# Transposing q, k, phi and x of the first six chunks on TensorE instead of by DMA

## The chip, the cores and the metric

One core of one Trainium2 chip runs the kernel. The metric is the device time of one execution in us. A profile holds one execution; its span goes from the first to the last instruction, and the execution's own time is somewhat longer.

## What is computed

q, k and v have shape (4, 8, 576, 64): four batches, eight heads, 576 positions, 64 features, float32. Attention with a memory is followed by two feed-forward layers over 2304 tokens (4 x 576) of width 512 (8 x 64):

```
scores = scale * q @ k^T, causal; a = softmax(scores); local = a @ v
q_p = phi(q), phi(x) = elu(x) + 1
mem_out = (q_p @ M_prev) / (q_p . z_prev + 1e-6)
x = g * mem_out + (1 - g) * local          # g = sigmoid(beta) per head
x = softplus(x @ moe_w_in) @ moe_w_out     # 512 -> 2048 -> 512
out = relu(x @ moe2_w_in)^2 @ moe2_w_out   # 512 -> 2048 -> 512
```

## The kernel before

**Precision.** Nearly every float32 operand is split in two 16-bit halves, a rounded one (hi) and the rest (lo), and the products are put together in PSUM. ScalarE makes hi with a Copy, VectorE makes lo with a subtraction.

**Chunks.** The tokens form 18 chunks of 128 (`g` = 0 to 17), nine for each pair of batches. For a chunk, `prep_k`, `prep_q`, `prep_phi` and `prep_v` (lines 201 to 247) take the loaded float32 tile, split it and bring it into the layout in which the features lie on partitions. For k, a head's 64 hi and 64 lo features stand side by side, so one 128 x 128 transpose per head gives `KT`. For q two orders are needed, hi-lo and lo-hi, as the score is the sum of (hi, lo) by (hi, lo) and of the swapped order: `qn` (line 203) has both orders, the second made by two VectorE copies (lines 206 and 207), and 16 blocks are transposed into `qT`. phi has eight blocks (`phiT`), x eight (`xT`), four of hi and four of lo.

**Transposes.** `transp(g, out, in_, lim)` (lines 186 to 199) has two routes. For `g >= lim` SP issues DMA transposes from SBUF to SBUF, 16 blocks in two halves, fewer at once (line 192). For `g < lim` TensorE transposes each block of 128 columns against an identity into a PSUM tile `tps` of eight blocks (line 198), and ScalarE copies the tile to SBUF (line 199). `TQ` is 2: q, k, x and the probabilities of chunks 0 and 1 go over TensorE, all later ones by DMA. phi has limit 0 and always goes by DMA.

**A chunk's attention.** A step is a group of one to four heads (`steps`, line 499). `emit_s` (lines 273 to 309): TensorE writes scores into the single tile `s_ps` (line 298), VectorE adds the mask and finds the row's extreme (line 302), ScalarE takes the exponential and its sum (line 306). `emit_p` (lines 311 to 325) splits the probabilities `Pt` into `p` (lines 319 and 320) and transposes them into `PT`. Four steps later (`LAG`) `emit_pv` (lines 327 to 344) multiplies `PT` by `V` and `phiT` by `Mt` into `pvt`; `prep_n` (line 249) makes the memory's norm. `emit_x` (lines 349 to 373) weighs and adds the two, splits x into `xn` and transposes it into `xT`, from which the first feed-forward layer reads. `attn_step` (line 535) emits the preparation of chunk g + 1 in four parts spread over the steps of chunk g.

**Feed-forward.** A block is two chunks (256 tokens). `unit_h` (line 411) multiplies `xT` by `W1` (`hps`, lines 421 to 423) and applies softplus on ScalarE and VectorE (lines 425 to 432); `unit_x` (line 444) and, for block 0, `unit_xq` (line 466) multiply by `W2`. The first layer's weights come in 32 pieces that are loaded by SP (lines 384 and 387) and split by VectorE and ScalarE (lines 403 to 408) while attention starts. The second layer (from line 681) follows when the first is done.

**What sets the order.** Each engine runs its own stream in order, and SP's queue issues loads, weight pieces and DMA transposes in order. A hand-written planner (lines 595 to 650) interleaves attention steps with units of feed-forward work from a queue, by estimated costs, and a scheduler orders each engine's stream when the program is built, by priorities set around `emit_s`, `emit_p`, `emit_x` and the weight pieces. PSUM has eight banks: `s_ps` two, `pvt` one, the accumulators of block 0 two, and `mm` three buffers, which `tps`, `nps` and `hps` share (line 96) until block 0 is done.

Of the kernel before, what the change touches and what calls it, by code (L numbers as in the profile page):

```python
# [9 lines left out]
F16 = mybir.dt.float16  # L10
# [3 lines left out]
AF = mybir.ActivationFunctionType  # L14
ALU = mybir.AluOpType
AX = mybir.AxisListType

P = 128
# [7 lines left out]

LOE = 99
TQ = 2
GPL = 0
W34P = 0  # L30

# [11 lines left out]
def kernel(  # L43
# [15 lines left out]
    pe, act, dve, pool, sp = nc.tensor, nc.scalar, nc.vector, nc.gpsimd, nc.sync  # L59
    B, H, S, D = q.shape  # L60
# [43 lines left out]
    att = att_cm.__enter__()  # L104
    sps = sps_cm.__enter__()
    pvp = pv_cm.__enter__()
    mm = mma_cm.__enter__()
# [25 lines left out]
    ident = stage.tile([P, P], F16, name="ident", bufs=1)  # L133
# [21 lines left out]
    raw, qT, phiT, KT, V, Mt, Pt, PT, pvt, cs_t = ({} for _ in range(10))  # L155
# [11 lines left out]
    def lo_eng(g):  # L167
        return dve if g < LOE else pool
# [17 lines left out]
    def transp(g, out, in_, lim):  # L186
        nblk = in_.shape[1] // P
        if g >= lim:
            step = nblk if nblk <= 12 else nblk // 2
            for a in range(0, nblk, step):  # L190
                e = a + step
                sp.dma_start_transpose(out=out[:, a:e], in_=in_[:, a * P:e * P])
            return
        for a in range(0, nblk, 8):
            e = min(nblk, a + 8)
            ps = mm.tile([P, 8, P], F16, tag="mm", name="tps")
            for i in range(a, e):
                pe.transpose(ps[:, i - a], in_[:, i * P:(i + 1) * P], ident)
            act.activation(out[:, a:e], ps[:, :e - a], AF.Copy)  # L199

    def prep_q(g):
        r = raw["q", g]
        qn = att.tile([P, 2, H, 2, D], F16, name="qn")
        act.activation(qn[:, 0, :, 0, :], r, AF.Copy)
        lo_eng(g).tensor_tensor(qn[:, 0, :, 1, :], r, qn[:, 0, :, 0, :], ALU.subtract)
        dve.tensor_copy(qn[:, 1, :, 1, :], qn[:, 0, :, 0, :])
        dve.tensor_copy(qn[:, 1, :, 0, :], qn[:, 0, :, 1, :])
        qT[g] = att.tile([P, 2 * H, P], F16, name="qT", bufs=2)
        transp(g, qT[g], qn.rearrange("p a h t d -> p (a h t d)"), TQ)

    def prep_k(g):
        r = raw.pop(("k", g))
        kn = att.tile([P, H, 2, D], F16, name="kn")
        act.activation(kn[:, :, 0, :], r, AF.Copy)
        lo_eng(g).tensor_tensor(kn[:, :, 1, :], r, kn[:, :, 0, :], ALU.subtract)
        KT[g] = att.tile([P, H, P], F16, name="KT", bufs=KVB)
        transp(g, KT[g], kn.rearrange("p h t d -> p (h t d)"), TQ)

    def prep_v(g):
        r = raw.pop(("v", g))  # L220
# [15 lines left out]
    def prep_phi(g):  # L236
        r = raw.pop(("q", g))
        e = att.tile([P, H, D], F32, tag="prod", name="phie")
        act.activation(e, r, AF.Relu, scale=-1.0)
        act.activation(e, e, AF.Exp, scale=-1.0)  # L240
        f = att.tile([P, H, D], F32, name="phi")
        dve.scalar_tensor_tensor(f, r, 0.0, e, ALU.max, ALU.add)
        fn = att.tile([P, H, 2, D], F16, name="phin")
        act.activation(fn[:, :, 0, :], f, AF.Copy)
        lo_eng(g).tensor_tensor(fn[:, :, 1, :], f, fn[:, :, 0, :], ALU.subtract)
        phiT[g] = att.tile([P, H, P], F16, name="phiT", bufs=2)
        transp(g, phiT[g], fn.rearrange("p h t d -> p (h t d)"), 0)

    def prep_n(g):
        ps = mm.tile([P, H], F32, tag="mm", name="nps")  # L250
# [60 lines left out]
    def emit_p(g, h0):  # L311
# [10 lines left out]
        nblk = G * 2 * w // P  # L322
        transp(g, t[:, :nblk], t16[:, :G * 2 * w], TQ)
        for i in range(G):
# [21 lines left out]
    xT = {}  # L346
    xf_t = {}

    def emit_x(g, a):
        kb, off = divmod(g * P, NB)  # L350
        if off == 0 and a == 0:
            xT[kb] = w1p.tile([P, 2 * NCC, NB], F16, name="xT", bufs=2)
        hs = slice(a * H // 2, (a + 1) * H // 2)
        cc = cc_t[g]
        c1 = cc[:, a, 0, :]
        dve.tensor_scalar(c1, cs_t[g][:, 1, hs], 1.0e-9, None, ALU.add)
        dve.reciprocal(c1, c1)
        dve.tensor_tensor(c1, c1, gP[:, hs], ALU.mult)
        t = att.tile([P, 2, H // 2, D], F32, tag="prod", name="xt")
        dve.tensor_tensor(  # L360
            t, pvt.pop(g),
            cc[:, a].rearrange("p t (h o) -> p t h o", o=1).to_broadcast([P, 2, H // 2, D]), ALU.mult,
        )
        if a == 0:
            xf_t[g] = att.tile([P, H, D], F32, name="xf")
        xf = xf_t[g]
        dve.tensor_tensor(xf[:, hs], t[:, 0], t[:, 1], ALU.add)
        if a == 0:
            return
        xn = att.tile([P, 2, H, D], F16, name="xn")  # L370
        act.activation(xn[:, 0], xf, AF.Copy)
        dve.tensor_tensor(xn[:, 1], xf, xn[:, 0], ALU.subtract)
        transp(g, xT[kb][:, :, off:off + P], xn.rearrange("p t h d -> p (t h d)"), TQ)


    NPC = 16
# [36 lines left out]
    def unit_h(kb, fp):  # L413
# [17 lines left out]
        act.activation(g[0], a, AF.Copy)  # L431
        (pool if fp % 8 < GPL else dve).tensor_tensor(g[1], a, g[0], ALU.subtract)  # L432

# [68 lines left out]
    def prep_part(g, part):  # L502
        if g >= NC:
            return
        if part == 0:
            prep_k(g)
            load("k", g + 1)
        elif part == 1:
            prep_q(g)
        elif part == 2:  # L510
            prep_phi(g)
            load("q", g + 1)
        elif part == 3:
            prep_v(g)
            load("v", g + 1)
            prep_m(g)
            load_m(g + 1)

    prep_k(0)
    prep_q(0)  # L520
    prep_phi(0)
    prep_v(0)
    load_m(0)
# [11 lines left out]
    def attn_step(s):  # L535
        if s < len(steps):
            g, h = steps[s]
            G = GRP[g % CPP]
            with tc.high_priority(HS):
                emit_s(g, h)  # L540
            nst = H // G
            i = h // G
            for part in range(4):
                if part * nst // 4 == i:
                    prep_part(g + 1, part)
            with tc.high_priority(HP):
                emit_p(g, h)
        for g, h0 in pv_at.get(s, ()):
            for h in range(h0, h0 + GRP[g % CPP]):
                emit_pv(g, h)  # L550
                if h % 4 == 3:
                    with tc.high_priority(HXE):
                        emit_x(g, h // 4)
# [131 lines left out]
    while t0 < NT:  # L685
# [7 lines left out]
        for f in range(NFC):  # L693
            ps = mm2.tile([P, 512], F32, tag="mm2", name="h2ps")
# [7 lines left out]
            r = bp.tile([P, 512], F32, name="r2", bufs=3)  # L702
            act.activation(r[:, :n], ps[:, :n], AF.Relu, scale=u2)  # L703
            act.activation(r[:, :n], r[:, :n], AF.Square)  # L704
            g = [bp.tile([P, 512], F16, name=f"gg{t}_{f}", bufs=1) for t in range(2)]
# [5 lines left out]
        for m in range(n // P):  # L711
            ps = mm2.tile([P, 512], F32, tag="mm2", name="ops")
# [39 lines left out]
```

## Time and profile before

| | |
|---|---|
| three runs | 1002.19, 1006.45, 1006.74 us; median 1006.45 |
| the profiled execution's own time | 1002.3 us |
| its span | 1000.5 us |
| TensorE busy | 923.6 us, 92% of the span |
| VectorE busy | 594.8 us |
| ScalarE busy | 550.4 us |
| DMA queue of SP | 103.84 MB, 51.6% of 16 engines' span |

The profile names engines PE (TensorE matmuls), PEld (its weight loads), DVE (VectorE), ACT (ScalarE), POOL (GpSimd) and SP (SyncE); a q behind a name is the engine's sequencer, which issues DMAs and waits. `out<-in` are the program's tile names, L298 is line 298 of the kernel. In a group of instructions `x32` is their number, then come busy us, the mean ns of one, and the idle time before them with what ended it. The chain of waits follows the work that ended last back from the end; shares of it are of the stretch asked for. DMA share is the mean busy share of 16 DMA engines; packets can overlap, so it can be over 1. PEclk is the granted TensorE clock as a share of full speed.

### The profile page before, as it was taken

The page shows a single profiled execution, that of the slowest core. Times are in us where ns is not written, and L with a number is a line of the kernel's source. Part 1 is how long each engine was busy: PE and PEld are TensorE (multiplying, and loading weights), DVE is VectorE, ACT ScalarE, POOL GpSimd, SP SyncE. Part 2 cuts the span into 40 slices and gives each one's busy share as a digit, 9 for nine tenths or more (in the row PEclk, how much of TensorE's full clock was granted, in tenths as well). Part 3 has the DMA queues.
Part 4 walks back from the last instruction along what each step waited for, and adds up shares of the span by engine and source line. Part 5 has one row for each costly group of instructions (what it writes and reads, how often), then busy time and mean ns, then how long its engine had stood idle before and what let it go on. Part 6 is the DMA issues. An engine that isn't in the chain of part 4 may idle for free.

```text
span 1000.5 us, 21041 instructions
## 1 busy us (share of the span) xinstructions
PE 923.6 (92%) x8594; PEld 678.8 (68%) x8612; DVE 594.8 (59%) x1376; ACT 550.4 (55%) x1102; POOL 2.9 (0%) x11
## 2 busy tenths in 40 slices
PE   3557689889999999999999999999999999999998
PEld 2346578778888888988888888864444444444483
DVE  7998889876756787786757499990240141042040
ACT  7756677777848688795948374650340241043040
POOL 1000000000000000000000000000000000000000
PEclk9998889999999999999999999999999999999999
DMA  9998998894867985598545366520000000000000
GB/s 225 231 213 173 181 199 166 176 162 73 133 118 122 170 161 104 94 171 139 98 75 99 54 211 195 183 86 22 22 1 21 22 1 11 32 1 1 32 11 22
DMA packets 299953, 105.21 MB, mean 105 GB/s; under 512 B 264784, under 2 KB 297552, under 8 KB 299856
## 3 DMA queue, kind: packets, MB, share of 16 engines
q1 hardware_dynamic: 299616, 103.84, 51.6%
q8 instruction: 67, 1.10, 0.5%
q14 instruction: 30, 0.25, 0.1%
q10 hardware_dynamic: 240, 0.02, 0.0%
HBM read 48.78 MB, written 4.72 MB: 53 GB/s over the span
## 4 chain that ended last, share of the span: by engine, by line
PE 70%; DVE 13%; DMA 10%; ACT 3%; issue 3%; SPq 1%; DVEq 0%; ACTq 0%
PE ops L717 7%; PE ops L715 6%; PE ops L716 6%; PE hps L421 5%; PE hps L422 5%; PE hps L423 5%; PE h2ps L700 5%; PE h2ps L699 5%; PE h2ps L701 5%; DMA PT<-p 4%; PE s_ps L298 4%; PE xps L439 4%; PE xps L438 4%; PE xps L440 4%; PE pvt L342 2%
## 5 line engine op out<-in xcount | busy, mean ns | idle before, releaser
L706 DVE CAST gg<-r 128x512 f16<-128x512 f32 (+1 forms) x80 | 32.0, 400 | 231.3 <-ACT r L704 205.0
L421 PE MATMUL hps<-xT,W 128*128 128x256 f16 x576 | 160.5, 279 | 6.3 <-ACT xT L199 4.1
L422 PE MATMUL hps<-xT,W 128*128 128x256 f16 x576 | 160.4, 278 | 0.0
L423 PE MATMUL hps<-xT,W 128*128 128x256 f16 x576 | 160.4, 278 | 0.0
L438 PE MATMUL xps<-g,W 128*128 128x256 f16 x512 | 138.9, 274 | 2.4 <-ACT g L431 2.4
L439 PE MATMUL xps<-g,W 128*128 128x256 f16 x512 | 139.5, 274 | 0.3 <-DVE g L432 0.3
L440 PE MATMUL xps<-g,W 128*128 128x256 f16 x512 | 139.5, 273 | 0.0
L306 ACT ACTIVATE Pt<-Pt,cs 128x128 f32<-128x128 f32 (+8 forms) x144 | 87.6, 608 | 57.1 <-DVE cs L302 57.1
L298 PE MATMUL s_ps<-KT,qT 128*128 128x128 f16 (+2 forms) x992 | 89.1, 225 | 27.0 <-DVE cs L302 25.0
L717 PE MATMUL ops<-W,gg 128*128 128x512 f16 x288 | 109.2, 379 | 0.9
L715 PE MATMUL ops<-W,gg 128*128 128x512 f16 x288 | 108.7, 379 | 1.2 <-ACT W L407 1.2
L719 ACT ACTIVATE osb<-ops 128x512 f32<-128x512 f32 x18 | 10.7, 597 | 169.8 <-PE ops L717 169.8
L302 DVE CUSTOM_DVE_ANT_0 Pt<-s_ps,mask 128x128 f32<-128x128 f32 (+8 forms) x144 | 79.6, 553 | 39.7 <-PE s_ps L298 39.0
L716 PE MATMUL ops<-W,gg 128*128 128x512 bf16 x270 | 102.3, 379 | 0.0
L700 PE MATMUL h2ps<-x,W 128*128 128x512 f16 (+1 forms) x256 | 90.2, 352 | 0.0
L701 PE MATMUL h2ps<-x,W 128*128 128x512 f16 (+1 forms) x256 | 90.2, 352 | 0.0
L699 PE MATMUL h2ps<-x,W 128*128 128x512 f16 (+1 forms) x256 | 90.2, 352 | 0.0
L298 PEld LDWEIGHTS <-qT 128*128 128x128 f16 x992 | 67.1, 104 | 33.9 <-issue 28.7
L320 DVE TENSOR_TENSOR p<-Pt,p 128x512 f16<-128x512 f32 (+5 forms) x116 | 75.1, 648 | 24.7 <-ACT p L319 24.2
L703 ACT ACTIVATE r<-h2ps 128x512 f32<-128x512 f32 (+1 forms) x80 | 44.1, 551 | 71.5 <-PE h2ps L701 71.4
L342 PE MATMUL pvt<-V,PT 128*128 128x64 f16 (+1 forms) x464 | 67.1, 201 | 12.6 <-DMA PT<-p 12.6
L319 ACT ACTIVATE p<-Pt 128x512 f16<-128x512 f32 (+5 forms) x116 | 68.9, 594 | 11.2 <-DMA PT<-p 9.7
(120 smaller groups left out, 1972.4 us busy)
## 6 DMA issues: line engine op xcount, KB each, us to landing
wst<-in_moe_w_in_dram SPq DMA_DIRECT2D x32, 512.0 KB, 4.8
wst<-in_moe_w_out_dram SPq DMA_DIRECT2D x32, 512.0 KB, 4.4
out_dram<-osb SPq DMA_DIRECT2D x18, 256.0 KB, 2.0
rawk<-in_k_dram SPq DMA_DIRECT2D x16, 256.0 KB, 4.6
rawq<-in_q_dram SPq DMA_DIRECT2D x16, 256.0 KB, 4.2
rawv<-in_v_dram SPq DMA_DIRECT2D x16, 256.0 KB, 3.7
PT<-p SPq DMA_TRANSPOSE x110, 3.4
mraw<-in_M_prev_dram SPq DMA_DIRECT2D x8, 128.0 KB, 3.6
```

Of the source, the lines that this page charges most:

```text
L298: pe.matmul(o, qT[g][:, t * H + h], KT[kb][:, h, k0:k0 + e - a], start=(t == 0), stop=(t == 1),)
L421: pe.matmul(o, wh, x[:, c], start=(c == 0), stop=False)
L422: pe.matmul(o, wh, x[:, NCC + c], start=False, stop=False)
L423: pe.matmul(o, wl, x[:, c], start=False, stop=(c == NCC - 1))
L438: pe.matmul(ps, wh, gh, start=(f == f0), stop=False)
L439: pe.matmul(ps, wh, gl, start=False, stop=False)
L440: pe.matmul(ps, wl, gh, start=False, stop=(f == f1 - 1))
L699: pe.matmul(ps[:, a - t0:e - t0], wh, xh, start=(c == 0), stop=False)
L700: pe.matmul(ps[:, a - t0:e - t0], wh, xl, start=False, stop=False)
L715: pe.matmul(ps, gh, W4[0][:, f, :], start=(f == 0), stop=False)
L716: pe.matmul(ps, gh, W4[1][:, f, :], start=False, stop=False)
L717: pe.matmul(ps, gl, W4[0][:, f, :], start=False, stop=(f == NFC - 1))
```

## The change

A new limit `TP` = 6 takes the place of `TQ` for q, k and x and of 0 for phi. The probabilities keep `TQ` = 2. For the first six chunks `prep_q` makes hi and lo once, transposes the eight blocks for the first half of `qT` as the others do, and gets the swapped order from 16 transposes of 64 columns each: the lo columns of a head go to partitions 0 to 63 of a second `tps` tile, the hi columns to 64 to 127, and ScalarE copies that tile to the second half of `qT`. The two VectorE copies are left out there.

```diff
--- before.py
+++ after.py
@@ -26,6 +26,7 @@
 
 LOE = 99
 TQ = 2
+TP = 6
 GPL = 0
 W34P = 0
 
@@ -200,13 +201,24 @@
 
     def prep_q(g):
         r = raw["q", g]
+        qT[g] = att.tile([P, 2 * H, P], F16, name="qT", bufs=2)
+        if g < TP:
+            qn = att.tile([P, H, 2, D], F16, tag="qn", name="qn")
+            act.activation(qn[:, :, 0, :], r, AF.Copy)
+            lo_eng(g).tensor_tensor(qn[:, :, 1, :], r, qn[:, :, 0, :], ALU.subtract)
+            transp(g, qT[g][:, :H], qn.rearrange("p h t d -> p (h t d)"), TP)
+            ps = mm.tile([P, H, P], F16, tag="mm", name="tps")
+            for h in range(H):
+                for t in range(2):
+                    pe.transpose(ps[t * D:(t + 1) * D, h], qn[:, h, 1 - t], ident)
+            act.activation(qT[g][:, H:], ps, AF.Copy)
+            return
         qn = att.tile([P, 2, H, 2, D], F16, name="qn")
         act.activation(qn[:, 0, :, 0, :], r, AF.Copy)
         lo_eng(g).tensor_tensor(qn[:, 0, :, 1, :], r, qn[:, 0, :, 0, :], ALU.subtract)
         dve.tensor_copy(qn[:, 1, :, 1, :], qn[:, 0, :, 0, :])
         dve.tensor_copy(qn[:, 1, :, 0, :], qn[:, 0, :, 1, :])
-        qT[g] = att.tile([P, 2 * H, P], F16, name="qT", bufs=2)
-        transp(g, qT[g], qn.rearrange("p a h t d -> p (a h t d)"), TQ)
+        transp(g, qT[g], qn.rearrange("p a h t d -> p (a h t d)"), TP)
 
     def prep_k(g):
         r = raw.pop(("k", g))
@@ -214,7 +226,7 @@
         act.activation(kn[:, :, 0, :], r, AF.Copy)
         lo_eng(g).tensor_tensor(kn[:, :, 1, :], r, kn[:, :, 0, :], ALU.subtract)
         KT[g] = att.tile([P, H, P], F16, name="KT", bufs=KVB)
-        transp(g, KT[g], kn.rearrange("p h t d -> p (h t d)"), TQ)
+        transp(g, KT[g], kn.rearrange("p h t d -> p (h t d)"), TP)
 
     def prep_v(g):
         r = raw.pop(("v", g))
@@ -244,7 +256,7 @@
         act.activation(fn[:, :, 0, :], f, AF.Copy)
         lo_eng(g).tensor_tensor(fn[:, :, 1, :], f, fn[:, :, 0, :], ALU.subtract)
         phiT[g] = att.tile([P, H, P], F16, name="phiT", bufs=2)
-        transp(g, phiT[g], fn.rearrange("p h t d -> p (h t d)"), 0)
+        transp(g, phiT[g], fn.rearrange("p h t d -> p (h t d)"), TP)
 
     def prep_n(g):
         ps = mm.tile([P, H], F32, tag="mm", name="nps")
@@ -370,7 +382,7 @@
         xn = att.tile([P, 2, H, D], F16, name="xn")
         act.activation(xn[:, 0], xf, AF.Copy)
         dve.tensor_tensor(xn[:, 1], xf, xn[:, 0], ALU.subtract)
-        transp(g, xT[kb][:, :, off:off + P], xn.rearrange("p t h d -> p (t h d)"), TQ)
+        transp(g, xT[kb][:, :, off:off + P], xn.rearrange("p t h d -> p (t h d)"), TP)
 
 
     NPC = 16
```

## Rows read from the trace of the kernel before

**Rows 1.** Busy time by stretch, all engines; columns in the first line.
```profile
core 0: us, PE busy (x) PEld busy (x) DVE busy (x) ACT busy (x) POOL busy (x), PEclk, DMA share, GB/s
0.00:50.00 50.00, 21.07 (x174) 15.10 (x175) 42.02 (x114) 38.80 (x82) 2.90 (x11) 1.00 1.09 228
50.00:75.00 25.00, 12.83 (x157) 10.95 (x156) 23.55 (x66) 14.74 (x33) 0.00 (x0) 1.00 0.98 213
75.00:125.00 50.00, 35.73 (x461) 30.38 (x459) 43.05 (x101) 31.40 (x62) 0.00 (x0) 0.86 0.87 177
125.00:225.00 100.00, 89.17 (x1035) 76.67 (x1034) 84.42 (x200) 72.16 (x152) 0.00 (x0) 0.93 0.92 176
225.00:1000.00 775.00, 764.81 (x6779) 545.69 (x6794) 401.79 (x900) 393.29 (x776) 0.00 (x0) 1.00 0.40 80
```

**Rows 2.** SP's transpose issues before 225 us: duration min/median/max ns, first and last start.
```profile
L192 SPq DMA_TRANSPOSE qT<-qn x13: 1238/1327/2780, 28.5 to 224.0; - x13
L192 SPq DMA_TRANSPOSE phiT<-phin x8: 1237/1664/3727, 14.2 to 221.3; - x8
L192 SPq DMA_TRANSPOSE KT<-kn x8: 1233/1639/2423, 22.2 to 191.2; - x8
L192 SPq DMA_TRANSPOSE xT<-xn x4: 1232/1234/1318, 109.8 to 214.3; - x4
```

**Rows 3.** Chain of waits, shares of the stretches 0 to 75 and 75 to 225 us.
```profile
by line: DMA rawq<-in_q_dram 12.6%; issue 8.2%; DMA rawv<-in_v_dram 8.0%; DMA PT<-p 5.4%; DMA rawk<-in_k_dram 4.8%; DVE Pt L302 4.5%; DMA mraw<-in_M_prev_dram 4.3%; DVE wcv L404 4.1%; ACT Pt L306 3.1%; DVE W L408 3.0%; DVE qn L205 2.7%; DVE
...
by line: DMA PT<-p 21.3%; PE hps L421 6.8%; PE hps L422 6.4%; PE hps L423 6.2%; PE s_ps L298 5.9%; issue 3.8%; PE xps L439 3.1%; PE xps L440 3.1%; PE pvt L342 3.1%; PE xps L438 3.1%; DMA xT<-xn 3.0%; PE xacc L478 2.7%; PE xacc L479 2.6%; PE
```

**Rows 4.** DMA view of 0 to 225 us: the queue, then issues, KB, us to landing.
```profile
q1 hardware_dynamic: 121291, 42.81, 94.8%
...
wst<-in_moe_w_in_dram SPq DMA_DIRECT2D x16, 512.0 KB, 5.5
...
rawk<-in_k_dram SPq DMA_DIRECT2D x11, 256.0 KB, 4.8
...
PT<-p SPq DMA_TRANSPOSE x35, 3.7
```

**Rows 5.** Busy time by stretch, 600 to 700 us; columns as in rows 1.
```profile
600.00:700.00 100.00, 98.66 (x745) 72.91 (x746) 73.72 (x139) 41.25 (x71) 0.00 (x0) 1.00 0.39 122
```

**Rows 6.** Single pieces of the chain of waits: start us, us, what.
```profile
1.25 5.11 DMA rawq<-in_q_dram
...
78.97 6.03 DMA PT<-p
```

**Rows 7.** DMA view of 225 to 600 us.
```profile
q1 hardware_dynamic: 164137, 44.80, 67.3%
...
PT<-p SPq DMA_TRANSPOSE x75, 3.3
```

**Rows 8.** Groups of instructions before 225 us: busy us, mean ns, idle before.
```profile
L198 PE MATMUL tps<-ident,qn 128*128 128x128 f16 x32 | 4.1, 309 | 2.1 <-DVE qn L205 0.8 <-DVE qn L207 0.8 <-ACT KT L199 0.5
...
L199 ACT ACTIVATE qT<-tps 128x1024 f16<-128x1024 f16 x4 | 4.0, 1010 | 0.0
...
L207 DVE COPY qn<-qn 128x512 f16<-128x512 f16 x9 | 2.6, 287 | 0.0
```

**Rows 9.** Who waited for whom before 225 us: us in total, times, longest.
```profile
DVE Pt L302 <- PE s_ps L298: 13.0, 10, 2.9
...
DVE kn L215 <- ACT kn L214: 5.6, 5, 1.5
...
DVE p L320 <- ACT p L319: 4.7, 6, 2.2
PE tps L198 <- ACT p L319: 4.3, 5, 1.1
...
PE hps L421 <- ACT xT L199: 4.1, 1, 4.1
```

## The prediction

> **What bounds the kernel now.** I began with busy time by stretch [rows 1]. From 225 us to the end TensorE is busy for 764.8 of 775 us. So from there on the time is TensorE's work, and nothing that the change touches lies there: its last transfer of x, that of chunk 5, is issued at 214.3 us [rows 2]. Before 225 us TensorE is busy for 21.1 + 12.8 + 35.7 + 89.2 = 158.8 us and idle for 66.2. What the change can win is a part of these 66 us; a front part that is shorter by some us brings the saturated part forward by as many.
>
> What holds the front part is not one engine. VectorE is busy for 42.0 + 23.6 + 43.1 + 84.4 = 193 of 225 us, and the DMA engines show a share of 0.87 to 1.09 in all four stretches, the highest of all [rows 1]. The chain of waits says where that ends last [rows 3]: in 0 to 75 us loads and transposes (rawq 12.6%, rawv 8.0%, PT 5.4%, rawk 4.8%, mraw 4.3%) with VectorE's lines between them, in 75 to 225 us PT's DMA transposes with 21.3% and xT's with 3.0%, between matmul groups of 6 to 7%. In us the first five are 9.4, 6.0, 4.0, 3.6 and 3.2, the last two 32.0 and 4.5. The transposes of q, k and phi are not among these names: they run a chunk ahead. They cost what they take from the same queue and the same DMA engines as the transfers that are waited for.
>
> **The change part by part.** Six chunks are touched; all that moves is issued before 225 us.
>
> 1. DMA transposes that go: phi of chunks 0 to 5 (6), q of chunks 2 to 5 in two halves (8), k (4) and x (4) of chunks 2 to 5, so 22 of the 33 transposes other than PT's that SP issues in this stretch [rows 2]. PT's 35 stay [rows 4]. Each of the 22 moves 128 x 1024 f16, 0.262 MB, in all 5.77 MB. Their price in DMA time: the queue takes 94.8% of 225 us, 213 us, for 42.81 MB [rows 4]. Loads in the same view are 32 pieces of W of 0.52 MB (16 of each source) and 29 loads of q, k and v of 0.26 MB, with 10 of half that, about 25.7 MB. At the rate of the late stretch where the queue carries little but weights (122 GB/s at a share of 0.39, so 313 GB/s [rows 5]) that is 82 us. The other 131 us went on 17.1 MB of transposes, 7.7 us for a MB: the 22 held about 44 us, 21% of the queue's time. The loads and PT that remain on the chain are 28.2 us in 0 to 75, less 5.1 for the first rawq, which lands before any transpose starts [rows 6], and 32.0 after: in all 53 us. In proportion they would shrink by 11 us. The other bound comes from the same operations later: in 225 to 600 us, where the queue's share is 67.3% and not 94.8%, PT lands in 3.3 us and not 3.7 [rows 4, 7]; that is 11% for a fall of 29%, so 8% or 4 us here. I take 9, near the upper end, because the pieces on the chain are not median ones but late ones, like the PT of 6.0 us [rows 6]. If landing doesn't follow the load at all it is 0.
>
> The Trainium skill, "DMA: Bandwidth & Descriptors", section "Latency and other measured facts", gives 261 GB/s for DMA transposes, twice the rate worked out above: by it the 22 held 22 us, 10% of the queue, and this term would be at most 5.5 us. No row here times a transpose alone, so the trace cannot decide between them; the case is like rival two.
>
> SP's queue also loses 22 issues of 1.2 to 3.7 us [rows 2], but waits charged to it are not among the chain's larger names, so I count nothing; should loads start earlier by that, it adds to the 9.
>
> 2. x of chunks 2 to 5: xT's DMA is 4.5 us on the chain. In its place come eight transposes and an eviction, 1.03 and 1.01 us (the rows of qn's 32 and of qT's evictions, shared out [rows 8]), with some wait for ScalarE, taken as 1 us: 3.0, a gain of 1.5. The bounds are a gain of 2.5 (no wait) and a loss of 1.6: one eviction of xT held an hps matmul for 4.1 us [rows 9].
>
> 3. VectorE: 12 copies (L206, L207 of six chunks) of 287 ns [rows 8] go, 3.4 us. VectorE is busy for 86% of the stretch, so most of it counts: 3.0, between 1 and 3.4.
>
> 4. TensorE: chunks 0 and 1 get 8 transposes for phi and 8 more for q each, 32; chunks 2 to 5 get 8 + 8 + 8 and, for q, 8 + 16, so 48 each, 192. Together 224. Eight of 128 columns take 1.03 us, and one alone 0.31, so each further one of a run takes 0.103 [rows 8]. No row has a transpose of 64 columns; between half of that price and the whole I take the whole, that of the nearest row, as the identity that streams past keeps its 128 columns. Half would save 5 us of TensorE's time. Total 23 us. By the times at which SP issued their DMAs, 168 of them fall before about 125 us, where TensorE is idle for 55 of 125 us, and 56 (q of chunk 5, phi of 5, x of 3, 4, 5) after it, where it is busy for 89 of 100 us. Beforehand: VectorE waited 13.0 us for s_ps in all [rows 9], 8% of TensorE's 158.8 busy us; 8% of 17.3 us is 1.4. Afterwards: the matmul lines named in the chain's row for 75 to 225 us add up to 43% of it [rows 3], and 43% of 5.8 us is 2.5. Cost 3.9, between 1.4 and 7.2. Cover for the rest is the 66 us of idle time.
>
> 5. ScalarE: new evictions are one each in chunks 0 and 1 (q's second half was evicted before too) and five in chunks 2 to 5: 22 x 1.005 = 22 us. ScalarE is busy for 157 of 225 us. Others waited for it for 5.6 + 4.7 + 4.3 + 4.1 = 18.7 us in the larger rows [rows 9], 12% of its busy time; 12% of 22 is 2.6. But nine of the evictions (phi of chunks 0 and 1, k of 2 to 4, q of 2 and 3) fall into the first 50 us, where it is busy for 38.8 already and nothing can start for about 5: full there. The bound above is thus 8; I take 3, as the prefetched k and q may wait.
>
> Sum: -9 - 1.5 - 3 + 3.9 + 3 = -6.6 us. The profiled execution took 1002.3 us (span 1000.5), so 995.7; the median of the three runs is 1006.45, 4 us above it. Against that median it is 999.85, and I say **1000**.
>
> **The rivals.** *Two: the queue was not what held PT.* A PT transpose has its own latency, which a free queue doesn't take away. Then term 1 is nought and -1.5 - 3 + 3.9 + 3 leaves +2.4: 1009, which cannot be told from no change. For it: PT's median landing hardly fell after 225 us [rows 7]. Against it: the chain's long pieces.
>
> *Three, slower: TensorE stands behind its own transposes.* It works in order. The 22 new tps tiles share three buffers with hps, nps and the tps of PT, and each is free only after an eviction on ScalarE, in its order too. The row of 4.1 us [rows 9] is this very wait. The point from which it decides: (6.6 + 5) / 22, so 0.5 us of mean wait for each tile makes the kernel slower by over 0.5%; at 0.8 us it is +17.6 - 6.6 = +11, 1017. For it: ScalarE's first 50 us. Against it: the four tps tiles of qn had 2.1 us of waiting in all [rows 8].
>
> *Four, a larger gain: DMA is the true bound of the front.* Then VectorE's idle time of 32 us shrinks by about 12, and with its 3.4 us it gives -15: 991. For it: the share of about 1 from 0 to 75 us. Against it: TensorE and ScalarE get 23 and 22 us more to do there.
>
> *Five: the clock.* The granted clock is 1.00 from 0 to 75 us, with TensorE busy for 33.9 of them, then 0.86 to 125 us and 0.93 to 225 us [rows 1]. That is some 28 of these 150 us at the lower of the two levels (1.2 and 2.4 GHz) after work with gaps. If transposes between matmuls bring as much again, at half speed with TensorE busy for 83%, it costs up to 12 us: +5.4, 1012. The Trainium skill, "TensorE: Matmul & The Clock Gate", section "Part 4: PE-mode transpose", says that transposes don't count as busy for the full clock; by that this rival would hold, while the stretches of 0 to 75 us, transposes among them, show 1.00 throughout and speak rather against it.
>
> That the change does not do what it says I exclude: every route for g < 6 is in the diff.
>
> **How the numbers follow.** Forecast 0.40, rival two 0.24, three 0.18, four 0.13, five 0.05. A measurement of this kernel tells about 0.5%, 5 us, from no change. Faster by more: 0.31 of the forecast's 0.40, all of four, 0.02 of two: 0.46. Within it: 0.09 + 0.19 + 0.03 of three: 0.31. Slower: 0.03 of two, 0.15 of three, five: 0.23. The range goes from 986 (rival four with landing's saving whole) to 1014, which holds rivals two and five and the start of three and leaves out some 2 in 10. The likeliest case's own range is 994 to 1006.
>
> **What would show it.** Right: PT's median landing before 225 us falls from 3.7 to about 3.3, its share of the chain from 21.3% to some 17%, the DMA share of the stretch to about 0.8, TensorE's idle time before the saturated part from 66 to near 36 (23 of work, 7 of gain). PE busy time rises by some 20 us, ScalarE's by 22, VectorE's falls by 3.4. Rival two: landing falls, the front part does not. Three: waits for ScalarE's L199 or for tps appear in TensorE's rows with over 11 us. Five: a granted clock under 0.90 there. A saturated part that starts later than 225 us, or is no longer saturated, would make the prediction wrong.

## The result, and the profile after

The changed kernel takes 1019.08 us (median of 4 runs, 1016.52 to 1019.92), the kernel before 1006.6 beside it (1002.19 to 1008.87). The ratio is 1.0135, with a 95% interval of 1.0105 to 1.0165: slower, where faster was forecast, and outside the range of 986 to 1014. The profiled execution took 1019.85 us, its span is 1018.0, against 1000.5. Two executions in a slow state, of 1592.6 us (the kernel before) and 1899.54 (e5 below, whose profile shows that one and is not used), are left out of every figure.

Busy time by stretch after, to be held against [rows 1]; the columns are the same.

```profile
0.00:50.00 50.00, 26.62 (x260) 20.82 (x260) 41.88 (x112) 44.24 (x93) 2.90 (x11) 0.95 0.83 195
50.00:75.00 25.00, 13.21 (x182) 11.83 (x183) 22.80 (x61) 16.02 (x31) 0.00 (x0) 0.57 0.65 161
75.00:125.00 50.00, 35.31 (x458) 29.89 (x458) 42.18 (x96) 35.44 (x66) 0.00 (x0) 0.75 0.80 164
125.00:225.00 100.00, 87.30 (x1030) 76.16 (x1030) 74.10 (x172) 69.48 (x141) 0.00 (x0) 0.90 0.72 140
225.00:1000.00 775.00, 762.27 (x6847) 548.16 (x6844) 410.60 (x926) 400.95 (x795) 0.00 (x0) 1.00 0.40 81
```

The front part did become lighter where the change took work away. The DMA share falls from 1.09, 0.98, 0.87 and 0.92 to 0.83, 0.65, 0.80 and 0.72, and VectorE has 181 us of work before 225 us instead of 193. TensorE is idle there for 62.6 us, against 66.2, though it was given more to do: whatever the transposes filled came back as idle time elsewhere. Over the whole span TensorE's busy time rose from 923.6 to 938.7 us and its idle time from 76.9 to 79.3. So the 17.5 us by which the span grew are 15.1 of added busy time and 2.4 of idle time: in sum nothing was covered. Only 3.6 of the 15.1 lie before 225 us; in exchange for the transposes, work that used to be done by then now follows later.

The chain of waits of 0 to 75 and of 75 to 225 us after, against [rows 3]:

```profile
by line: DMA PT<-p 11.1%; DVE wcv L416 8.9%; issue 8.2%; DVE p L332 7.3%; DVE wcv L417 7.3%; DVE Pt L314 6.8%; DMA rawq<-in_q_dram 6.8%; DVE W L420 5.5%; DVE wcv L415 5.0%; DMA rawv<-in_v_dram 4.6%; DVE V L235 4.1%; DVE xt L372 2.4%; DVE ph
...
by line: DMA PT<-p 10.9%; DMA rawk<-in_k_dram 6.2%; issue 6.1%; DMA rawv<-in_v_dram 5.2%; DVE p L332 4.3%; PE hps L433 3.9%; PE hps L435 3.7%; PE hps L434 3.7%; DVE Pt L314 3.1%; DMA rawq<-in_q_dram 2.7%; DVE wcv L416 2.6%; ACT Pt L318 2.4%
```

PT's share in the second stretch is halved, from 21.3% to 10.9%, xT's is gone, and the time did not follow: "issue", rawk, rawv and VectorE's lines take the place. In the first stretch PT's share rose, from 5.4% to 11.1%. The DMA view of the first 225 us after, against [rows 4]:

```profile
q1 hardware_dynamic: 92768, 35.73, 75.0%
...
PT<-p SPq DMA_TRANSPOSE x31, 3.8
```

The queue's share fell from 94.8% to 75.0%, and PT's median landing did not fall at all: 3.8 us, 3.7 before. Of the signs that the forecast named, the lower DMA share and the lower share of PT from 75 us on came; the shorter landing, and an idle time of 36 us before the saturated part, did not.

Who TensorE's transposes and first-layer matmuls waited for before 225 us, after, against the last two of [rows 9]:

```profile
PE tps L199 <- ACT KT L200: 3.4, 1, 3.4
...
PE hps L433 <- ACT phiT L200: 2.9, 2, 1.9
...
PE tps L199 <- DVE phin L257: 1.4, 1, 1.4
...
PE tps L199 <- DVE p L332: 1.0, 2, 0.6
...
PE tps L199 <- ACT p L331: 0.8, 3, 0.3
PE tps L199 <- ACT phiT L200: 0.8, 1, 0.8
...
PE tps L213 <- ACT KT L200: 0.5, 1, 0.5
PE tps L199 <- ACT xn L383: 0.4, 1, 0.4
```

These waits are 11.2 us, and 11.6 with two of 0.2. Before, the same kind of rows had 15.7 us, 8.4 of them in [rows 9]. Those that are for ScalarE's evictions (L200, before L199) are 7.6 of the 11.6, before 4.6 of the 15.7: 3 us more, and the sum is lower. So TensorE does not stand in front of these instructions longer than it did. What happens is seen when the busy time is asked for the first layer's tile alone (hps: 24 matmuls a unit, then ScalarE and VectorE). Before:

```profile
core 0: us, PE busy (x) DVE busy (x) ACT busy (x), PEclk, DMA share, GB/s
75.00:110.00 35.00, 11.21 (x72) 2.05 (x3) 1.77 (x3) 0.87 0.89 181
110.00:140.00 30.00, 10.01 (x72) 0.68 (x1) 1.74 (x3) 0.82 0.85 185
140.00:185.00 45.00, 18.40 (x144) 4.77 (x7) 3.51 (x6) 0.96 0.97 185
185.00:230.00 45.00, 12.44 (x95) 2.24 (x4) 1.77 (x3) 0.92 0.87 154
```

After:

```profile
75.00:110.00 35.00, 8.06 (x48) 1.36 (x2) 1.19 (x2) 0.70 0.75 149
110.00:140.00 30.00, 0.00 (x0) 0.00 (x0) 0.00 (x0) 0.78 0.92 196
140.00:185.00 45.00, 25.35 (x210) 4.79 (x7) 4.64 (x8) 0.95 0.87 169
185.00:230.00 45.00, 9.15 (x81) 3.45 (x5) 2.33 (x4) 0.92 0.46 83
```

From 110 to 140 us the first layer does nothing, where the kernel before ran three units. In one stretch from 0 to 230 us, in which no matmul is counted twice at a border, first before, then after:

```profile
0.00:230.00 230.00, 52.06 (x383) 9.74 (x15) 8.79 (x15) 0.93 0.95 191
0.00:230.00 230.00, 42.56 (x336) 9.60 (x14) 8.16 (x14) 0.84 0.74 158
```

That is 16 units (one matmul has no record) and 14. Attention meanwhile is early: VectorE's scores of chunk 5 end at 194 us, not 201. Then comes the bill: those of chunk 8 end at 312 us, not 296. That the units which were not run, and now have to be run while attention needs TensorE too, are the reason is read from this order of events and was not tested. Some of it shows as waiting. From 185 to 225 us after, in us in total:

```profile
DVE spa L440 <- ACT spa L439: 8.8, 3, 7.6
ACT V L234 <- DMA rawv<-in_v_dram: 8.3, 3, 5.4
DVE V L235 <- ACT V L234: 7.8, 3, 5.3
```

The V loads of the next chunks, whose buffers come free only when pv of chunk 4 is done, came late (ScalarE starts on the V of chunk 6 at 192 us, 181 before; pv of chunk 4 is used up by VectorE at 193, 183 before), and ScalarE and VectorE, in order, stood behind them.

### The profile page after: what moved, and what is told of

The parts are those of the page before. It is cut to its first block, busy times and chain, and to the rows that moved or that the text cites. A ratio compares the mean times of both kernels' runs of the same rounds, so it can differ in the third digit from the quotient of the medians.

```text
span 1018.0 us, 21454 instructions
## 1 busy us (share of the span) xinstructions
PE 938.7 (92%) x8836; PEld 693.0 (68%) x8836; DVE 591.6 (58%) x1364; ACT 567.3 (56%) x1124; POOL 2.9 (0%) x11
## 4 chain that ended last, share of the span: by engine, by line
PE 63%; DVE 17%; DMA 10%; ACT 5%; issue 4%; SPq 1%; ACTq 0%; DVEq 0%
PE ops L727 6%; PE ops L729 6%; PE ops L728 6%; PE h2ps L713 5%; PE h2ps L711 5%; PE h2ps L712 5%; PE hps L433 4%; PE hps L435 4%; PE hps L434 4%; DMA PT<-p 3%; PE xps L451 3%; PE xps L450 3%; PE xps L452 3%; PE s_ps L310 3%; DVE wcv L416 3%
## 5 line engine op out<-in xcount | busy, mean ns | idle before, releaser
L728 PE MATMUL ops<-W,gg 128*128 128x512 bf16 x288 | 109.2, 379 | 0.0
```

The source lines that it names most:

```text
L728: pe.matmul(ps, gh, W4[1][:, f, :], start=False, stop=False)
```

## The experiments

Each was timed beside the kernel before, whose median moved between 1003 and 1007 us, so ratios to it are compared; kernels are edits of the changed kernel unless the text says otherwise, and are called e1 to e15 after their expectations' names.

**The four that tell the theories apart.** In the first (e1) the new tiles get a PSUM bank that mm gives up:

```diff
-    mma_cm = tc.tile_pool(name="mma", bufs=3, space=PSUM, reuse_waits="tile")
+    mma_cm = tc.tile_pool(name="mma", bufs=2, space=PSUM, reuse_waits="tile")
+    tpp_cm = tc.tile_pool(name="tpp", bufs=1, space=PSUM, reuse_waits="tile")
...
-            ps = mm.tile([P, 8, P], F16, tag="mm", name="tps")
+            ps = (tpp if lim == TP else mm).tile([P, 8, P], F16, tag="mm", name="tps")
...
-            ps = mm.tile([P, H, P], F16, tag="mm", name="tps")
+            ps = tpp.tile([P, H, P], F16, tag="mm", name="tps")
...
```

> The changed kernel, but the tps tiles of q, k, phi and x get a PSUM bank of their own and leave nps, hps and the tps of PT two of the three mm buffers. Theory A (buffers): the new tps tiles sit in the same rotation of three buffers as nps and hps, so nps and the first layer's hps units stand behind the next chunk's preparation; with a bank of their own the norm of chunk 4 is back at about 126 us (150.7 in the changed kernel) and the time falls to 1000 to 1009 us, in spite of the buffer that mm lost. Theory B (work): TensorE is the bound and the 15 us of busy time that it gained simply add; where the tiles lie does not matter: 1016 us or more. Theory C (clock): the stretches at half clock, 77 us against 32 recorded, cost the time: they stay and so does the time, 1016 us or more.

Measured: 997.24 us beside 1003.14, ratio 0.9938 (0.9918 to 0.9958), 3 us under theory A's range. The second (e2) has the two buffers without the new bank (the first line of that diff alone):

> Control of the first: the changed kernel with only two mm buffers and a bank left empty. Theory A: the rotation gets tighter, nps and hps fall back further, 1022 us or more. Theories B and C: the same work, so about 1017 to 1021 us.

Measured: 1024.68 us, 1.0212 (1.0191 to 1.0233). With the same instructions and the same two buffers for nps and hps, a bank of their own for the transposes is worth 27 us. Theory B falls. Theory C, the clock, is not settled by this pair, because the recorded clock moved with the time (75 to 125 us: 0.85 in e1, 0.77 in e2); it is taken up under rival five below.

The third (e3) keeps q's part alone, the fourth (e4) all but phi's:

```diff
-        transp(g, KT[g], kn.rearrange("p h t d -> p (h t d)"), TP)
+        transp(g, KT[g], kn.rearrange("p h t d -> p (h t d)"), TQ)     # e3
-        transp(g, phiT[g], fn.rearrange("p h t d -> p (h t d)"), TP)
+        transp(g, phiT[g], fn.rearrange("p h t d -> p (h t d)"), 0)     # e3, e4
-        transp(g, xT[kb][:, :, off:off + P], xn.rearrange("p t h d -> p (t h d)"), TP)
+        transp(g, xT[kb][:, :, off:off + P], xn.rearrange("p t h d -> p (t h d)"), TQ)     # e3
```

> Only q's part of the change (chunks 0 to 5, the swapped order by 64-column transposes); k and x at limit 2 and phi by DMA as before. 8 DMA transposes go, 112 transposes and 8 evictions come, 12 VectorE copies go. Theory A: fewer tiles stand ahead of nps, and q's two are taken early in a chunk; about 1002 to 1008 us. Theory B: half of the transposes, so half of the loss, about 1012 us. Theory C: by the clock, which could be any.

> The changed kernel with phi by DMA again. phi's tile is the one that is emitted right ahead of the norm of the chunk before, at the same step. Theory A: much of the lag of nps goes, 1005 to 1013 us. Theory B: 48 of 224 transposes and 6 of 22 evictions fewer, a fifth of the loss, about 1015 us. Theory C: about as the changed kernel.

Measured: q alone 993.62 us, 0.9906 (0.9883 to 0.9929), better than either theory said; without phi 1009.82 us, 1.0066 (1.0045 to 1.0087). In e4's hps rows the first layer falls back later than in the changed kernel:

```profile
110.00:140.00 30.00, 9.20 (x71) 0.68 (x1) 1.17 (x2) 0.83 0.96 190
...
185.00:230.00 45.00, 5.68 (x48) 1.38 (x2) 1.17 (x2) 0.85 0.45 80
```

Three units run from 110 to 140 us, but only 48 matmuls after 185, where the kernel before has 95; by 230 us they are 336 again.

**Which part costs what.** With q alone as the base, one more part at a time, k in e5 and x in e6:

> q's part and k's (chunks 0 to 5), x at limit 2 and phi by DMA; four more tps tiles than q alone. Theory A (tiles that stand ahead of nps and hps in mm's rotation): k's tile is taken at the first step of a chunk, four steps ahead of the norm, so little is lost: 994 to 1000 us, at most 6 us over q alone. A rival (any further tile costs alike, by its work): 22 tiles minus 8 cost 1019 - 994 = 25 us, so 1.8 us a tile, and four of them give 1001 us.

Measured: 998.09 us beside 1005.85, 0.9928 (0.9904 to 0.9951); by its ratio 2 us over q alone, with intervals that overlap.

> q's part and x's (chunks 0 to 5), k at limit 2 and phi by DMA; again four tiles more than q alone. Theory A: x's tile waits for a whole chain of VectorE and ScalarE work while it holds its place ahead of hps units, so it costs more than k's: 1002 to 1010 us. The rival (any tile alike): 1001 us, as with k.

Measured: 1003.65 us, 0.9979 (0.9964 to 0.9993): 7 us over q alone. The two parts have the same number of tiles, so a price for each tile by its work does not hold. Nor has a part one price. By the ratios x costs 7 us beside q, 14 beside q and k (e4 against e5); k 2 beside q, 9 beside q and x (e4 against e6); phi 10 beside q and k (e13 below against e5), 7 beside all the others (the changed kernel against e4), and still 5, at the edge of the noise, where the tiles have their own bank (e1 against e12 below). So not all of phi's price is the rotation's.

**The terms of the sum, one by one, in q alone.** Transposes of q made twice into the same tile (e7), and evictions made twice (e8):

```diff
+            for _ in range(2):
                 for h in range(H):
                     pe.transpose(ps[:, h], ..., ident)         # e7
...
+                for _ in range(2):
                     act.activation(qT[g][...], ps, AF.Copy)    # e8
```

> q alone, with each transpose of q done twice into the same tile: 144 more transposes in chunks 0 to 5, no further tile and no further eviction. Theory A: most lie where TensorE is idle, 1 to 5 us over q alone, 995 to 999 us. Theory B (the work counts in full): 144 x 0.1 us, so 1008 us.

Measured: 1002.77 us, 0.9968 (0.9948 to 0.9987): 6 us over q alone for 144 transposes, between the two theories.

> q alone, with each eviction of q's tiles done twice: 12 more evictions of 1.0 us on ScalarE, and each tile held for 1 us longer. By the prediction's 12 to 14% of ScalarE's time 1.6 us over q alone; a ScalarE that is full in the first 50 us would make it 4 to 12: 998 to 1006 us.

Measured: 996.46 us, 0.9911 (0.9881 to 0.9942): 0.5 us over q alone, not to be told from none.

Then what q's part had taken away was put back, six DMA transposes in e10, the copies in e11:

```diff
+            scr = att.tile([P, H, P], F16, name="scr")         # e10
+            sp.dma_start_transpose(out=scr, in_=qn.rearrange("p h t d -> p (h t d)"))
...
+            dve.tensor_copy(scr[:, :, 1, :], qn[:, :, 0, :])   # e11
+            dve.tensor_copy(scr[:, :, 0, :], qn[:, :, 1, :])
```

> q alone, with one DMA transpose of 0.26 MB in each of chunks 0 to 5 issued besides, into a tile that nothing reads: 6 of the 8 transposes that q's part took off the queue. What DMA's relief is worth: by the prediction's term 1, 9 us for 22, so 2.5 us over q alone (996); by rival two 0 to 0.5 us (993.6 to 994).

Measured: 994.08 us beside 1004.0, 0.9900 (0.9870 to 0.9929), no slower than q alone. The DMA view of the first 225 us, first q alone:

```profile
q1 hardware_dynamic: 115760, 41.43, 90.4%
...
PT<-p SPq DMA_TRANSPOSE x36, 3.9
```

and with the six transposes back:

```profile
q1 hardware_dynamic: 122096, 43.00, 97.5%
...
PT<-p SPq DMA_TRANSPOSE x36, 3.8
```

The queue is 7 points fuller, PT lands no later, and the time stays. The two intervals still leave room for the 2.5 us of term 1. And since nothing reads the new tile, the run tests the load alone, and not what attention gains when it need not wait for q's own DMA transposes.

> q alone, with the two VectorE copies of each of the six chunks made besides, into a tile that nothing reads: 12 x 0.287 us. By the prediction's term 3, 3 us over q alone (996.6), between 1 and 3.4; if VectorE does not hold the front part, 0.

Measured: 996.91 us, 0.9933 (0.9906 to 0.9961): by the ratios 2.7 us, as forecast, though the intervals overlap.

These four do not explain why q alone is faster. An estimate from them: its 112 added transposes at e7's price are +4.7 us, its 8 evictions at e8's +0.3, the copies -2.7, the queue's load 0, in sum +2.3, where q alone measured -9.4. Some 12 us of gain stay open. That attention no longer waits for these transposes (qT's DMA landed in a median of 4.0 us before) is one candidate, which no run tests.

**Who stands behind whom.** e9 is the changed kernel with the chunk's norm emitted early:

```diff
+            if h == 0:
+                prep_n(g)
             nst = H // G
...
-        if h == 0:
-            prep_n(g)
         if h % 4 == 0:
```

> The changed kernel with the norm of a chunk emitted at the chunk's first step, ahead of the next chunk's preparation, in the same three mm buffers. Theory A1 (the norm, and with it pvt, x and SP's queue, is what stands behind the preparation): 1000 to 1008 us. Theory A2 (it is the hps units of the first layer, which still stand behind tps tiles in the rotation): 1012 us or more.

Measured: 1015.46 us, 1.0113 (1.0077 to 1.0150). By the total this is A2's case. The trace does not bear the total out. e9's hps rows:

```profile
110.00:140.00 30.00, 10.02 (x79) 0.68 (x1) 1.18 (x2) 0.83 0.83 168
...
0.00:230.00 230.00, 42.40 (x336) 9.59 (x14) 8.26 (x14) 0.86 0.76 163
```

With the norm early, 79 matmuls run from 110 to 140 us, more than before the change, and the scores of chunk 8 end at 298 us (before 296, after 312); but the span is 1014.3 us. Most of e9's loss comes after that point, so its total cannot tell A1 from A2. The rows say one thing more: e9, e4 and e15 (below; 70 matmuls) fill the gap from 110 to 140 us and are slower than the kernel before all the same. That gap alone is not what costs the time. The mark that all slower kernels share comes later: by 230 us they have run 336 matmuls of the first layer (the changed kernel, e4, e9, e13, e14, e15) or 312 (e2), while the kernel before and all faster ones with a profile have run 383 to 410.

Next, x back to DMA (e13: limit `TQ` for xT alone), and the own bank for x's tiles alone or for those of q, k and phi alone (the tpp line of e1 for those calls):

> The changed kernel with x of chunks 2 to 5 by DMA again; q, k and phi on TensorE in the shared three buffers. Theory X (x's tile, which waits for a whole chunk's attention, is what the hps units stand behind): 1004 us or less. Theory R (the next chunk's q, k and phi tiles do it as well): 1008 to 1016 us.

> The changed kernel with a bank of its own for x's tps tiles alone; q, k, phi, nps and hps share two mm buffers. Theory X: 1000 to 1008 us. Theory R: 1013 to 1024 us, by the two buffers nearer to 1024.

> The changed kernel with a bank of its own for the tps tiles of q, k and phi; x, nps and hps share two mm buffers. Theory X: x's tile still stands ahead of hps, 1012 us or more. Theory R: most of the loss goes, 995 to 1005 us.

Measured: e13 1008.31 us, 1.0029 (1.0009 to 1.0049); e14 1021.22, 1.0162 (1.0139 to 1.0185); e15 1015.22, 1.0099 (1.0071 to 1.0126). e13 and e14 say R, e15 says X. Against their common control with two buffers, 1.0212, x's bank is worth 0.5%, that of the others 1.1%, and one bank for all 2.7%: either kind of tile left in the rotation keeps most of the loss. Standing in it is not a loss by itself: q alone and e5 have q's tiles, and q's and k's, in the same three buffers and are faster than the kernel before.

The programs' own order shows what stands ahead of what. In all kernels in which one pool serves tps, nps and hps, TensorE's stream takes the pool's tiles exactly in the order in which the program asks for them; in e1, e12, e14 and e15 alone some are overtaken. Between the second and the third unit of the first layer, in the order of the stream:

```
before   hps 2 | nps 3 | hps 3
after    hps 2 | tps x2 | tps phi4 | nps 3 | tps k5 | tps q5 | tps q5 | tps x3 | hps 3
```

The third unit needs none of these tiles. But it is asked for after x3, and x3 is ready only when chunk 3's attention is through: its transposes end at about 142 us in the trace after, and hps starts in that moment. k5, q5 and phi4 are prefetch, which is ready when loads, ScalarE and VectorE get to it. With DMA transposes none of them was in the rotation. What is shown is that the shared pool costs the time (e1 against e2, e12 against e4). That it is the order, and not the lack of free buffers, is argued from the waits, whose sum did not grow; a bank of their own changes both, and which of the units that are held up costs the time no run shows.

**A version that beats both.** In e12, q, k and x with their own bank, phi by DMA (e1's diff and e4's):

> q, k and x on TensorE with a bank of their own for tps (two mm buffers for the rest), phi by DMA as before. Theory A: without its own bank this was 1009.8 us; with it the units come early, 990 to 998 us. Theory B: no change from 1009.8.

Measured: 992.88 us beside 1004.0, 0.9888 (0.9858 to 0.9919). The same without the own bank is e4, at 1.0066. Its hps rows:

```profile
75.00:110.00 35.00, 13.08 (x94) 2.06 (x3) 1.73 (x3) 0.90 0.95 197
110.00:140.00 30.00, 9.57 (x67) 2.05 (x3) 1.77 (x3) 0.89 0.80 171
140.00:185.00 45.00, 16.82 (x131) 4.11 (x6) 3.51 (x6) 0.92 1.03 192
185.00:230.00 45.00, 13.97 (x122) 3.28 (x5) 2.96 (x5) 1.00 0.53 95
```

and its busy time by stretch:

```profile
0.00:50.00 50.00, 24.53 (x252) 18.86 (x252) 42.99 (x117) 43.46 (x91) 2.90 (x11) 0.84 0.94 214
50.00:75.00 25.00, 16.37 (x242) 14.99 (x243) 24.24 (x65) 17.21 (x35) 0.00 (x0) 0.63 0.78 161
75.00:125.00 50.00, 45.71 (x618) 40.36 (x618) 47.11 (x106) 42.48 (x81) 0.00 (x0) 0.93 0.87 181
125.00:225.00 100.00, 81.91 (x973) 69.84 (x971) 80.91 (x196) 73.84 (x155) 0.00 (x0) 0.93 0.84 159
225.00:1000.00 775.00, 757.59 (x6711) 538.28 (x6708) 394.93 (x883) 385.36 (x761) 0.00 (x0) 1.00 0.40 79
```

By 230 us it has run 410 matmuls of the first layer. TensorE is busy for 45.7 of the 50 us from 75 on, where before and after it had 35.7 and 35.3. Of e12 and q alone neither can be called the faster: their intervals overlap.

## Why the prediction was wrong

The step that failed is the sentence under term 4, "Cover for the rest is the 66 us of idle time", with what the sum rests on: that the first layer's units keep their places while the transposes fill gaps. The new tiles were priced as work and, in rival three, as waits for an eviction. That they are asked for in the same rotation as hps, and that TensorE takes a pool's tiles in that order when the stream is built, was in no term. In place of the cover, TensorE's idle time rose from 76.9 to 79.3 us and its busy time by 15.1. With a bank of their own for the new tiles (e1) the whole change measured 0.6% faster, some 6 us; with the shared rotation it measured 1.35% slower, and 2.1% with e1's two buffers (e2). That e1's 6 us are also the sum's 6.6 is chance, since the terms were off one by one.

Term by term:
1. DMA relief, taken as 9: no gain is seen. e10 put six of q's eight transposes back for nothing, within its noise, and after, PT's landing did not fall with the queue's share. That speaks for the lower bound, 0, and for rival two, and against the proportional rule; that late pieces shrink with the load is what I took without a row. In the working, 28.2 us should read 26.2; the 53 us that follow are right.
2. x, taken as a gain of 1.5: in the shared rotation it costs 7 us (e6 against e3).
3. VectorE's copies, taken as 3.0: 2.7 in e11, not clear of noise.
4. TensorE's work: 6 us (with some 3 of noise) for 144 transposes in e7, where the term's share for so many would be 2.5 (3.9 x 144 / 224). It was too low by more than half; by the median e7's own forecast of 1 to 5 us misses too. The price of a transpose, though, was too high. The rows after (start us, us):

```profile
120.04 0.61 PE L199 MATMUL tps<-ident,phin 128*128 128x128 f16 x8
...
123.36 0.64 PE L213 MATMUL tps<-ident,qn 128*64 128x128 f16 x16
```

Eight of 128 columns take 0.61 us here, not 1.03, and sixteen of 64 columns take 0.64. In the trace these sixteen start in pairs, 3 ns apart, with some 53 ns from pair to pair, and each lasts 0.22 us, as a full one does: the two of a head, which write different halves of the partitions, run side by side. So a pair costs what one full transpose does, and "the whole" for each was the wrong choice; what one alone would cost no run shows.
5. ScalarE: 12 evictions cost 0.5 us in e8, where 3 x 12 / 22 = 1.6 was the share; the noise does not tell these apart. The first 50 us did fill up (44.2 us busy), with no effect that can be told.

Rival three named the right place, the three buffers that tps, nps and hps share, and the right sign. That its 1017 us lie near the 1019 is luck: they came from a mean wait of 0.8 us for each new tile, and such waits are not in the rows. Rival four did not come. Rival five, the clock, is not shown to be the cause. From 85 to 225 us, where each of these profiles has records of the clock, the granted clock was 0.87 after and 0.90 before, so it did fall a little. But e14 and e6 have the same clock there:

```profile
85.00:225.00 140.00, 118.10 (x1479) 102.04 (x1479) 109.98 (x260) 102.49 (x204) 0.00 (x0) 0.91 0.73 150
85.00:225.00 140.00, 122.82 (x1511) 105.67 (x1511) 118.53 (x280) 105.74 (x217) 0.00 (x0) 0.91 0.82 165
```

and e14 is 1.6% slower than the kernel before, e6 0.2% faster. q alone has 0.78 from 75 to 125 us, near the 0.75 after, and is 0.9% faster. What part of the 1.35% the clock makes stays open. The Trainium skill ("TensorE: Matmul & The Clock Gate", "Part 4: PE-mode transpose") says that transposes don't count as busy for the full clock. e7, which doubles q's transposes, has 0.58 from 45 to 75 us where q alone has 0.61: that they do not raise the clock here agrees as far as it goes, and no run shows that this costs time by itself.

## What to carry to other kernels

Before moving work to TensorE, ask which pool its output tile comes from and who else asks for that pool's tiles: in the streams of this program a tile that is ready late stands ahead of all that ask after it, even if they need nothing of it. Count the order as well as the work; where idle time is to be filled, the work of the stage that follows must be able to pass. A bank of its own for such tiles was worth more here than a third buffer for the others.

## What the runs showed of the hardware

PT's DMA transposes landed in a median of 3.7 to 3.9 us whether the queue's share of the first 225 us was 75.0%, 90.4%, 94.8% or 97.5%. Two transposes of 64 columns that write different halves of the partitions run side by side, as told under term 4. And a granted clock of 1.00 early in the trace need not mean the upper level. In the kernel before this row stands in a stretch of [rows 1] with 1.00:

```profile
8.59 1.03 PE L198 MATMUL tps<-ident,kn 128*128 128x128 f16 x8
```

while after, the eight transposes of 0.61 us lie in this one:

```profile
120.00:124.00 4.00, 3.23 (x75) 2.96 (x72) 3.83 (x10) 3.98 (x7) 0.00 (x0) 1.00 0.80 197
```

In the trace each further transpose of a run starts 0.107 us after the last in the first and 0.055 us in the second. One is twice the other, as the two levels are (1.2 and 2.4 GHz): the first row ran at the lower level under a listed 1.00. The first record of the clock stands at 83.5 us before, at 41.7 after, at 39.2 in q alone and at 12.3 in e7, and what is listed ahead of it is 1.00 in all four. So the listed clock cannot be compared between kernels in the first 75 us, and the prediction's reading of those rows for rival five was empty.
